# Attention, weight conversions and the first unit's products: finishing the second pair of tiles before the third is begun

## The chip, the cores and the metric

The kernel runs on one core of one Trainium2 chip. The metric is the device time of one execution in microseconds, as the median of several runs. The core has five engines with an instruction list each, worked off in order: TensorE (PE, matmuls and transposes), VectorE (DVE), ScalarE (ACT), GpSimd (POOL) and SyncE (SP, which here only issues loads and stores).

## The reference

Three stages follow each other. All arrays are float32 at the result; the weights of the second stage arrive as 64-bit floats.

```python
# 1: softmax attention inside chunks of 64 positions; q, k, v are (8, 8, 576, 64)
scores = scale * np.matmul(q_c, k_c.transpose(0, 1, 2, 4, 3))
attn = np.exp(scores - np.max(scores, axis=-1, keepdims=True))
attn = attn / (np.sum(attn, axis=-1, keepdims=True) + 1e-09)
out = np.matmul(attn, v_c)                      # -> x, (8, 576, 512)
# 2: token shift and channel mix; w_k 512x1024, w_v 1024x512, w_r 512x512
x_prev = np.concatenate([np.zeros((B, 1, D)), x[:, :-1, :]], axis=1)
xk = mu_k * x + (1.0 - mu_k) * x_prev
xr = mu_r * x + (1.0 - mu_r) * x_prev
k = np.maximum(xk @ w_k, 0.0)
v = k * k @ w_v
r = 1.0 / (1.0 + np.exp(-(xr @ w_r)))
x = r * v
# 3: four causal attention experts on x, the two best per token mixed by their gates
```

## The kernel before

`attn_mix` computes the first two stages, `experts` the third. The 4608 tokens are 36 tiles of 128 tokens for the attention and 12 units of 384 tokens (three tiles) for the mix.

**Attention.** Tiles are taken in pairs j. `s_T` turns q and k of one tile (four 128x128 transposes each on PE, a copy on ACT, L129), and issues the load of q and k two tiles on. `s_S` makes the scores of a pair (32 matmuls of 64x64, L154) and the softmax on DVE and ACT. `s_PT` turns the probabilities of one tile. `s_PV` multiplies by v (32 matmuls, L184), copies the result into the unit's tile XT on ACT (L44), and issues the loads of v two tiles on (four issues each, L113). `s_prev` (POOL) sets the column before a unit. These steps stand in the list `attn`; before the change, pair j's turn is: `s_T` of its two tiles, `s_PT` of the two tiles of pair j-1, then `s_SPV`, which is `s_S` of pair j and `s_PV` of pair j-1. So pair j-1 is finished only behind the transposes and scores of pair j.

**Mix.** `s_shift` makes, for one of four groups of 128 features, xr or xk of a unit: ACT scales the earlier tokens (L239), DVE adds the present ones (L240), ACT rounds to the high part (xhr or xhk, L243), and DVE subtracts for the low part (xlr or xlk, L244). Unit 0 needs XT of tiles 0 to 2, so both pair 0 and pair 1 must be finished. A product of high and low parts is three matmuls of 128x384 (L57 to L59). A unit is four `mix_r` (12 matmuls each, then a sigmoid on ACT, L257), eight `mix_k` (12 each) and four `mix_v` (24 each): 240 matmuls. The products go into three PSUM buffers named mps.

**Conversions.** Twenty pieces of 128x512 weights (four of w_r, eight of w_k, eight of w_v) go through `conv`: a load of 512 KB into `st` (L304), the absolute value on ACT into `cz` (L310), a maximum on POOL (L311), three integer operations on DVE (L312 to L314), the high part on POOL (L46) and the low part on DVE (L324, into wrl, wkl or wvl). There are two buffers of `cz` and two of `st`; the first four pieces use, as `st`, the tiles that later hold xhr, xlr, xhk and xlk.

**Order.** The program is written as one string of steps: CFG['pro'] for the opening (c a conversion, q and v loads, a an attention step, s the first unit's shift, ahead of which `attended(0)` runs all attention steps that unit 0 needs), and then the units' products with the rest among them: in unit 0 `early=(2, 1)` conversions per product item, and a running credit (rate0 for units 0 and 1, then rate) that releases one attention step when it reaches 1. A scheduler then lays out each engine's list from that order and from its own timing model, so the lists do not follow the string exactly.

Of the kernel before, what the change touches and what calls it, by code (L numbers as in the profile page):

```python
# [8 lines left out]
F32 = mybir.dt.float32  # L9
F32R = mybir.dt.float32r  # L10
I32 = mybir.dt.int32
# [8 lines left out]

CH = 64
UNIT = 384
CFG = dict(ps=(2, 3, 1, 2), P=5, sm=3, load=6, lag=(3, 4), out=(5, 1), qk1=(1, 1), qk0=(10, 1.2), v=(11, 1), order=(3, 4, 0, 1, 2), after=1, conv='v', clo='v', chi='g', x2hi='g', x2lo='v', ylo='g', yhi='v', xt='aa', r2='av', klo='vg', amul='vg', nearly=2, x2b=1, yb=4, qb=4, direct=((0, 1), (1, 1), (1, 1)), tailAV=4, kp=1, yt=1, yf=2, zb=1, om=(4, 3, 2, 1, 0), hp=1000, x2d=2, early=(2, 1), dact=3, rate0=0.43, rate=0.45, sh=(10, 12, 2), sh2=(11, 1, -1), pro='cccqqaacavvcaaaaacaacaaaascc', alag=2, seq=0, end=2, outL=(13, 2), outE=2, kcp='aa', dsc='v', ldb=2, vb=2, cn=512, stb=2, xb=4, pa=5, tb=2, first_j=7)
SEG = 192


# [22 lines left out]
def f32(ap):  # L49
    return ap.bitcast(F32)  # L50
# [11 lines left out]
def attn_mix(tc, at, x2T, q, k, v, mu_k, mu_r, w_k, w_v, w_r, ident, attended_all, mixed_k):  # L62
# [9 lines left out]
    TPU = UNIT // 128  # L72
# [4 lines left out]
    with ExitStack() as ctx:  # L77
        wts = ctx.enter_context(tc.tile_pool(name="wts", bufs=1))
        mx = ctx.enter_context(tc.tile_pool(name="mx", bufs=1))
        ps = ctx.enter_context(tc.tile_pool(name="psM", bufs=1, space=PSUM))  # L80

        pa_open = ExitStack()
        pa = pa_open.enter_context(tc.tile_pool(name="psA", bufs=1, space=PSUM, side="right"))
        wkr_open = ExitStack()
        wkr = wkr_open.enter_context(tc.tile_pool(name="wkr", bufs=1, side="right"))
# [9 lines left out]
        def runs(t):  # L95
            b, s = divmod(t * 128, S)
            return [(0, b, s, 128)] if s + 128 <= S else [(0, b, s, CH), (CH, b + 1, 0, CH)]

        def load_qk(t):
            for src, nm in ((q, "q"), (k, "k")):  # L100
                x = at.tile([128, H * D], F32, tag="ld" + nm, bufs=CFG["ldb"], name="ld" + nm)
                for p, b, s, n in runs(t):
                    nc.sync.dma_start(out=x[p:p + n].rearrange("p (h d) -> p h d", h=H),
                                      in_=src[b, :, s:s + n, :].rearrange("h p d -> p h d"))
                qkv[nm, t] = x

        def load_v(t):
            x = at.tile([128, 2, HP, D], F32, tag="ldv", bufs=CFG["vb"], name="ldv")
            for c in range(2):
                b, s = divmod(t * 128 + c * CH, S)  # L110
                for e in range(2):
                    r = e ^ c
                    nc.sync.dma_start(out=x[r * 64:(r + 1) * 64, c],  # L113
                                      in_=v[b, e::2, s:s + CH, :].rearrange("g p d -> p g d"))
            qkv["v", t] = x

        qT, kT, PP, PT, XT = {}, {}, {}, {}, {}
        nT = NU * TPU

        def bank(nm):  # L120
            return pa.tile([128, HP, 128], F32, tag="A", bufs=CFG["pa"], name=nm)

        def to_sbuf(src, nm):

            p = bank("Tps")
            for g in range(HP):
                nc.tensor.transpose(p[:, g], src[:, g * 128:(g + 1) * 128], ident)  # L127
            o = at.tile([128, HP, 128], F32, tag=nm, bufs=CFG["tb"], name=nm)
            nc.scalar.activation(out=o, in_=p, func=ACTF.Copy)  # L129
            return o  # L130

        def s_T(t):
            qT[t] = to_sbuf(qkv.pop(("q", t)), "qT")
            kT[t] = to_sbuf(qkv.pop(("k", t)), "kT")
            if t + CFG["ldb"] < nT:
                load_qk(t + CFG["ldb"])

# [6 lines left out]
        def s_S(j):  # L144
            banks = [bank("Sps").rearrange("p g (i k) -> p i g k", i=2) for _ in range(2)]
            for i in range(2):
                a, b = qT.pop(2 * j + i), kT.pop(2 * j + i)
                for g in range(HP):
                    for c in range(2):
                        for o in range(2):  # L150
                            e = o ^ c
                            r, cc = slice(e * 64, e * 64 + 64), slice(c * CH, (c + 1) * CH)
                            with tc.high_priority(1000) if j < CFG["first_j"] else nullcontext():
                                nc.tensor.matmul(out=banks[o][cc, i, g], lhsT=a[r, g, cc], rhs=b[r, g, cc],  # L154
                                                 start=True, stop=True)
            m = at.tile([128, 2, 2, HP], F32, tag="m", name="m")
            e = at.tile([128, 2, HP, 2, CH], F32, tag="P", name="P")
            for o, p in enumerate(banks):
                nc.vector.tensor_reduce(m[:, o], p, axis=AXX, op=ALU.max)
                nc.vector.tensor_tensor(e[:, :, :, o], p, m[:, o].unsqueeze(3).to_broadcast([128, 2, HP, CH]),  # L160
                                        op=ALU.subtract)
            ef = e.rearrange("p i g o k -> p (i g o) k")
            nc.scalar.activation(out=ef, in_=ef, func=ACTF.Exp, scale=scale)
            z = m.rearrange("p o i g -> p (o i g)")
            nc.vector.tensor_reduce(z, ef, axis=AXX, op=ALU.add)
            nc.vector.tensor_scalar(z, z, 1e-9, None, op0=ALU.add)
            nc.vector.reciprocal(z, z)
            eng(nc, CFG["amul"][j >= CFG["first_j"]]).tensor_tensor(
                ef, ef, z.unsqueeze(2).to_broadcast([128, 2 * H, CH]), op=ALU.mult)
            for i in range(2):  # L170
                PP[2 * j + i] = e[:, i]
# [33 lines left out]
        def s_SPV(j):  # L205
            if 2 * j < nT:
                s_S(j)
            if j:
                s_PV(j - 1)

        def s_prev(u):
# [84 lines left out]
        def conv(src, dst, g, c0, n):  # L296

            i = done[0] - 1
            if i < 4:

                st = wkr.tile([128, n, 2], I32, tag=("xhr", "xlr", "xhk", "xlk")[i], name="st")
            else:
                st = at.tile([128, n, 2], I32, tag="st", bufs=CFG["stb"], name="st")
            nc.sync.dma_start(out=st.rearrange("p f w -> p (f w)"),  # L304
                              in_=src.bitcast(I32)[g * 128:(g + 1) * 128, 2 * c0:2 * (c0 + n)])
            h, l = st[:, :, 1], st[:, :, 0]
            z = at.tile([128, n], F32, tag="cz", bufs=2, name="cz")
            b = z.bitcast(I32)

            nc.scalar.activation(out=z, in_=f32(h), func=ACTF.Abs)  # L310
            nc.gpsimd.tensor_scalar(z, z, F64_ZERO, None, op0=ALU.max)  # L311
            nc.vector.tensor_scalar(b, b, 3, 0x3FFFFFF8, op0=ALU.logical_shift_left, op1=ALU.bitwise_and)  # L312
            nc.vector.scalar_tensor_tensor(b, l, 29, b, op0=ALU.logical_shift_right, op1=ALU.bitwise_or)
            nc.vector.scalar_tensor_tensor(b, h, -(1 << 30), b, op0=ALU.bitwise_and, op1=ALU.bitwise_or)  # L314
            split(z, dst, g, c0, n)
# [6 lines left out]
        def split(z, dst, g, c0, n):  # L322
            copy(nc, CFG["chi"], dst.hi[:, g, c0:c0 + n], z)
            eng(nc, nth(CFG["clo"], done[0])).tensor_tensor(dst.lo[:, g, c0:c0 + n], z, f32(dst.hi[:, g, c0:c0 + n]), op=ALU.subtract)  # L324
# [12 lines left out]
        attn = []  # L337
        for j in range(nT // 2 + 1):
            two = (2 * j, 2 * j + 1)
            attn += [(t // TPU, s_T, t) for t in two if t < nT]  # L340
            attn += [((t - 2) // TPU, s_PT, t - 2) for t in two if t > 1]
            attn.append(((2 * j - 1) // TPU if j else 0, s_SPV, j))
            attn += [(t // TPU, s_prev, t // TPU) for t in (2 * j - 2, 2 * j - 1) if t > 0 and t % TPU == TPU - 1]
        attn.reverse()

        def attend(u, n=1):
# [22 lines left out]
        loads = {"q": iter(range(CFG["ldb"])), "v": iter(range(CFG["vb"]))}  # L369

        def first_shift():
            for ws in ((1, 0),) if CFG["sh2"][2] >= 0 else ((1,), (0,)):
                for g in range(KD):
                    s_shift(0, ws, g)

        for c in CFG["pro"]:
            if c == "a":
                attend(2)
            elif c == "c":
                convert(1)  # L380
            elif c in loads:
                (load_qk if c == "q" else load_v)(next(loads[c]))
            else:
                attended(0)
                first_shift()

        credit = 0.0
        for u in range(NU):
# [6 lines left out]
            for i, (f, *args) in enumerate(items):  # L395
# [10 lines left out]
                if u + 1 < NU:  # L406
                    both = u + 1 <= CFG["sh2"][2]
                    for ws, at0 in (((1, 0), CFG["sh2"][0]),) if both else (((1,), CFG["sh"][0]), ((0,), CFG["sh"][1])):
                        g, r = divmod(i - at0, CFG["sh2" if both else "sh"][1 if both else 2])
# [481 lines left out]
```

## Time and profile before

| | |
|---|---|
| median of 3 runs | 1044.99 us (1044.38 to 1045.49) |
| profiled execution | 1048.14 us |
| its span | 1046.4 us |
| PE busy | 993.4 us, 95% |
| DVE busy | 721.5 us, 69% |
| ACT busy | 586.5 us, 56% |
| POOL busy | 413.7 us, 40% |

The span runs from the first to the last instruction of the trace; the execution's own time lies 1.74 us above it, and 3.15 us above the median. PE is the busy engine, so the reading goes by where PE is not busy or runs below full clock, and then by what it waits for there: the windows, then the waits, then the chain of work that ended last, and then the engines' own timelines.

### The profile page before, as it was taken

How to read it: one execution, taken by the hardware profiler on the slowest of the kernel's cores; microseconds unless marked ns; L12 is line 12 of the kernel's file. 1: busy time of each engine (PE TensorE's matmuls, PEld its weight loads, DVE VectorE, ACT ScalarE, POOL GpSimd, SP SyncE). 2: the span in 40 equal slices, each digit the busy share in tenths (PEclk: the TensorE clock that was granted, in tenths of full speed). 3: DMA queues.
4: the chain of work that ended last, by engine and by line, in shares of the span. 5: the costliest groups of instructions: out<-in, count | busy, mean ns of one | idle time of the engine just before them, and what ended most of it. 6: DMA issues, size and time to landing. Idle time of an engine off the chain costs nothing.

```text
span 1046.4 us, 22262 instructions
## 1 busy us (share of the span) xinstructions
PE 993.4 (95%) x8422; PEld 953.4 (91%) x8422; DVE 721.5 (69%) x1793; ACT 586.5 (56%) x1379; POOL 413.7 (40%) x507
## 2 busy tenths in 40 slices
PE   3679899999999999999999999999999999999997
PEld 2569899998999999999999999999989998999986
DVE  5899835537654856565666632688787787878996
ACT  3378573545354545454453412477676776777675
POOL 5443303526443755464554537433332423313101
PEclk8589999999999999999999999999999999999999
DMA  9774522152324242323213125454452645253312
GB/s 230 188 197 122 126 57 81 41 122 62 86 58 109 54 122 49 99 72 87 56 47 81 31 61 131 107 145 119 103 155 58 181 72 158 63 156 108 103 34 92
DMA packets 167522, 105.27 MB, mean 101 GB/s; under 512 B 133512, under 2 KB 145912, under 8 KB 167416
## 3 DMA queue, kind: packets, MB, share of 16 engines
q1 hardware_dynamic: 132024, 54.55, 20.3%
q0 software_dynamic: 35392, 49.30, 18.2%
q8 instruction: 67, 1.10, 0.5%
q14 instruction: 39, 0.32, 0.1%
HBM read 66.01 MB, written 28.38 MB: 90 GB/s over the span
## 4 chain that ended last, share of the span: by engine, by line
PE 68%; DVE 18%; ACT 4%; DMA 4%; issue 3%; POOL 2%; SPq 1%; ACTq 0%; DVEq 0%; POOLq 0%
PE mps L57 12%; PE mps L59 12%; PE mps L58 12%; PE pj L57 5%; PE pj L58 5%; PE pj L59 5%; PE Tps L663 4%; PE Tps L127 3%; PE AVps L687 2%; PE AVps L683 2%; PE Sps L603 2%; PE Sps L602 2%; DVE r L271 2%; DVE sm L605 1%; PE Sps L154 1%
## 5 line engine op out<-in xcount | busy, mean ns | idle before, releaser
L57 PE MATMUL mps<-xhk,wkh 128*128 128x384 f32 x384 | 131.8, 344 | 0.1
L57 PE MATMUL mps<-kh,wvh 128*128 128x384 f32 x384 | 129.8, 342 | 1.1 <-DVE x2o L288 0.9
L58 PE MATMUL mps<-kl,wvh 128*128 128x384 f32 x384 | 128.4, 336 | 2.5 <-POOL kl L273 2.4
L58 PE MATMUL mps<-xlk,wkh 128*128 128x384 f32 x384 | 129.1, 337 | 0.0
L59 PE MATMUL mps<-xhk,wkl 128*128 128x384 f32 x384 | 128.9, 336 | 0.0
L59 PE MATMUL mps<-kh,wvl 128*128 128x384 f32 x384 | 127.0, 336 | 0.9 <-DVE wvl L324 0.9
L271 DVE TENSOR_TENSOR r<-r 128x384 f32<-128x384 f32 x80 | 65.8, 823 | 85.8 <-ACT r L264 85.8
L273 POOL TENSOR_TENSOR kl<-r,kh 128x384 fp32r<-128x384 f32 x80 | 87.7, 1100 | 83.0 <-ACT kh L272 81.9
L615 ACT ACTIVATE P<-sm,nm 128x128 f32<-128x128 f32 (+4 forms) x160 | 91.3, 571 | 36.9 <-DVE nm L609 20.2
L605 DVE CUSTOM_DVE_ANT_0 sm<-Sps,mask 128x192 f32<-128x192 f32 (+3 forms) x192 | 83.6, 438 | 18.5 <-PE Sps L603 16.9
L228 POOL TENSOR_TENSOR xa<-XT 128x384 f32<-128x384 f32 x72 | 71.0, 994 | 60.3 <-DVE xlr L244 34.9
L272 ACT ACTIVATE kh<-r 128x384 fp32r<-128x384 f32 x96 | 50.7, 529 | 59.5 <-DVE r L271 59.0
L663 PE MATMUL Tps<-ident,P 128*128 128x128 f32 x480 | 80.8, 275 | 1.4 <-DVE PT03l L667 0.5
L242 DVE SCALAR_TENSOR_TENSOR xa<-xa,mu,XT 128x384 f32<-128x384 f32 x72 | 67.2, 949 | 15.4 <-POOL xa L228 15.4
L58 PEld LDWEIGHTS mps<-kl,wvh 128*128 128x128 f32 x384 | 72.1, 188 | 4.0 <-POOL kl L273 4.0
L57 PEld LDWEIGHTS mps<-kh,wvh 128*128 128x128 f32 x384 | 71.9, 188 | 2.7 <-DVE x2o L288 1.2
L57 PEld LDWEIGHTS mps<-xhk,wkh 128*128 128x128 f32 x384 | 72.5, 189 | 1.0 <-ACT r L264 0.7
L524 POOL DMA_DIRECT2D K<-Kp x64 | 34.2, 553 | 98.7 <-ACT Kp L517 98.1
L59 PEld LDWEIGHTS mps<-kh,wvl 128*128 128x128 f32 x384 | 71.8, 188 | 1.2 <-DVE wvl L324 1.2
L58 PEld LDWEIGHTS mps<-xlk,wkh 128*128 128x128 f32 x384 | 72.3, 188 | 0.1
L57 PE MATMUL mps<-xhr,wrh 128*128 128x384 f32 x192 | 66.7, 349 | 5.8 <-ACT sig L257 3.3
L59 PEld LDWEIGHTS mps<-xhk,wkl 128*128 128x128 f32 x384 | 72.2, 188 | 0.0
(202 smaller groups left out, 2914.9 us busy)
## 6 DMA issues: line engine op xcount, KB each, us to landing
x2T<-x2d POOLq DMA_DIRECT2D x48, 384.0 KB, 3.2
x<-x2T POOLq DMA_DIRECT2D x32, 576.0 KB, 6.4
ldv<-in_v_dram SPq DMA_DIRECT2D x144, 64.0 KB
K<-Kp POOLq DMA_DIRECT2D x64, 144.0 KB, 3.0
ldq<-in_q_dram SPq DMA_DIRECT2D x32, 256.0 KB
ldk<-in_k_dram SPq DMA_DIRECT2D x32, 256.0 KB
out_dram<-o SPq DMA_DIRECT2D x32, 256.0 KB
st<-in_moe_w_k_dram SPq DMA_DIRECT2D x8, 512.0 KB
```

Of the source, the lines that this page charges most:

```text
L57: nc.tensor.matmul(out=out, lhsT=ah, rhs=bh, start=first and i == 0, stop=False)
L58: nc.tensor.matmul(out=out, lhsT=ah, rhs=bl, start=False, stop=False)
L59: nc.tensor.matmul(out=out, lhsT=al, rhs=bh, start=False, stop=last and i == n - 1)
L228: nc.gpsimd.tensor_tensor(d, now, prev, op=ALU.subtract)
L242: nc.vector.scalar_tensor_tensor(a, d, m, prev, op0=ALU.mult, op1=ALU.add)
L271: eng(nc, CFG["r2"][u >= CFG["nearly"]]).tensor_tensor(r2, r, r, op=ALU.mult)
L272: nc.scalar.activation(out=o.hi, in_=r2, func=ACTF.Copy)
L273: eng(nc, CFG["klo"][u >= CFG["nearly"]]).tensor_tensor(o.lo, r2, f32(o.hi), op=ALU.subtract)
L524: nc.gpsimd.dma_start(out=d[half[j]], in_=t[half[i]])
L605: nc.vector.tensor_tensor_reduce(out=sm[:n, a:a + w], in0=pp[:n, :w], in1=mk[:, a:a + w], op0=ALU.add, op1=ALU.min, scale=-scale, scalar=3e38,
L615: nc.scalar.activation(out=x[:n, :nk], in_=sm[:n, :nk], func=ACTF.Exp, scale=-1.0, bias=nm[:n, :1], accum_out=z)
L663: nc.tensor.transpose(pp[:, j - j0], x[:, o:o + 128], ident)
```

## The change

Five edits, all in `attn_mix` and its settings:

- in the list `attn`, pair 1 is finished ahead of pair 2: its two `s_PT`, its `s_PV` and unit 0's `s_prev` stand before `s_T` of tiles 4 and 5, and the turn of j = 2 then holds only `s_S`, with unit 1's tag;
- the opening string has 7 conversions and 12 attention steps ahead of the first shift's s where it had 9 and 14 (two more conversions and two more attention steps follow in before: its string ends `aaaaacaacaaaascc`, the new one `aaaaaccaaaas`);
- rate0 goes from 0.43 to 0.5;
- the first four conversions keep their value in a third part of the tile that holds their `st`, and take no `cz` buffer;
- `first_shift` always makes xk of all four groups and xr of all four apart. With the settings here it did that already.

Code below the edit moves down by one to six lines: L304 becomes L306, L310 to L314 become L311 to L315, L324 becomes L325.

```diff
-CFG = dict(
...
-rate0=0.43, pro='cccqqaacavvcaaaaacaacaaaascc',
+rate0=0.5, pro='cccqqaacavvcaaaaaccaaaas',
...
         def s_SPV(j):
             if 2 * j < nT:
                 s_S(j)
-            if j:
+            if j and j != 2:
                 s_PV(j - 1)
...
             if i < 4:
-                st = wkr.tile([128, n, 2], I32, tag=("xhr", "xlr", "xhk", "xlk")[i], name="st")
+                x = wkr.tile([128, 3 * n], I32, tag=("xhr", "xlr", "xhk", "xlk")[i], name="st")
+                st, z = x[:, :2 * n].rearrange("p (f w) -> p f w", w=2), f32(x[:, 2 * n:])
             else:
+                z = at.tile([128, n], F32, tag="cz", bufs=2, name="cz")
                 st = at.tile([128, n, 2], I32, tag="st", bufs=CFG["stb"], name="st")
...
-            z = at.tile([128, n], F32, tag="cz", bufs=2, name="cz")
...
-            attn += [(t // TPU, s_T, t) for t in two if t < nT]
-            attn += [((t - 2) // TPU, s_PT, t - 2) for t in two if t > 1]
-            attn.append(((2 * j - 1) // TPU if j else 0, s_SPV, j))
-            attn += [(t // TPU, s_prev, t // TPU) for t in (2 * j - 2, 2 * j - 1) if t > 0 and t % TPU == TPU - 1]
+            turned = [((t - 2) // TPU, s_PT, t - 2) for t in two if t > 1]
+            prevs = [(t // TPU, s_prev, t // TPU) for t in (2 * j - 2, 2 * j - 1) if t > 0 and t % TPU == TPU - 1]
+            if j == 2:
+                attn += turned + [(0, s_PV, 1)] + prevs
+                turned, prevs = [], []
+            attn += [(t // TPU, s_T, t) for t in two if t < nT] + turned
+            attn.append(((2 * j - 1) // TPU if j and j != 2 else 2 * j // TPU, s_SPV, j))
+            attn += prevs
...
-            for ws in ((1, 0),) if CFG["sh2"][2] >= 0 else ((1,), (0,)):
+            for ws in ((1,), (0,)):
```

The lists hold the same instructions in total, but for two more loads of an ACT table (25 for 23). Three places where the order differs follow; rows read line, operation, output and inputs, shape and a count. The first is ACT's list around the four copies (L44) that complete unit 0's XT: before, then after.

```order
L310 ACTIVATE cz<-st 128x512
L129 ACTIVATE PT<-Tps 128x512
L163 ACTIVATE P<-P 128x1024
L129 ACTIVATE qT<-Tps 128x512
L310 ACTIVATE cz<-st 128x512
L44 ACTIVATE XT<-PVps 128x4x64 x4
L239 ACTIVATE xb<-XT,mu_94 128x384 x2
L129 ACTIVATE kT<-Tps 128x512
L129 ACTIVATE qT<-Tps 128x512
L310 ACTIVATE cz<-st 128x512
L129 ACTIVATE kT<-Tps 128x512
L243 ACTIVATE xhr<-xb 128x384
```

```order
L311 ACTIVATE cz<-st 128x512
L129 ACTIVATE PT<-Tps 128x512 x2
L311 ACTIVATE cz<-st 128x512 x2
L44 ACTIVATE XT<-PVps 128x4x64 x4
L129 ACTIVATE qT<-Tps 128x512
L239 ACTIVATE xb<-XT,mu_94 128x384 x2
L129 ACTIVATE kT<-Tps 128x512
L129 ACTIVATE qT<-Tps 128x512
L243 ACTIVATE xhr<-xb 128x384
```

Before, the copies stand behind the absolute value of the eleventh conversion, and that of the twelfth stands between them and the first xhr; after, those of the eleventh and twelfth both stand ahead of the copies, and none between the copies and the first xhr.

The second is DVE's list around the first shift (the first L240 and the first L244), before and then after.

```order
L313 SCALAR_TENSOR_TENSOR cz<-st,cz 128x512
L314 SCALAR_TENSOR_TENSOR cz<-st,cz 128x512
L165 TENSOR_REDUCE m<-P 128x16
L166 TENSOR_SCALAR m<-m 128x16
L167 RECIPROCAL m<-m 128x16
L168 TENSOR_TENSOR P<-P,m 128x1024
L324 TENSOR_TENSOR wkl<-cz,wkh 128x512
L240 SCALAR_TENSOR_TENSOR xb<-XT,mu,xb 128x384 x2
L312 TENSOR_SCALAR cz<-cz 128x512
L313 SCALAR_TENSOR_TENSOR cz<-st,cz 128x512
L244 TENSOR_TENSOR xlr<-xb,xhr 128x384
```

```order
L325 TENSOR_TENSOR wkl<-cz,wkh 128x512 x2
L313 TENSOR_SCALAR cz<-cz 128x512
L314 SCALAR_TENSOR_TENSOR cz<-st,cz 128x512
L315 SCALAR_TENSOR_TENSOR cz<-st,cz 128x512
L313 TENSOR_SCALAR cz<-cz 128x512
L240 SCALAR_TENSOR_TENSOR xb<-XT,mu,xb 128x384
L314 SCALAR_TENSOR_TENSOR cz<-st,cz 128x512
L240 SCALAR_TENSOR_TENSOR xb<-XT,mu,xb 128x384
L315 SCALAR_TENSOR_TENSOR cz<-st,cz 128x512
L244 TENSOR_TENSOR xlr<-xb,xhr 128x384
```

Before, the last softmax of the opening and one conversion stand ahead of the first L240; after, no softmax stands there, and the twelfth conversion's operations are spread around the two L240.

The third is PE's list up to the first products (rhs xhr), before and then after.

```order
L127 MATMUL Tps<-ident,ldk 128x128 x4
L127 MATMUL Tps<-ident,ldq 128x128 x4
L127 MATMUL Tps<-ident,ldk 128x128 x4
L127 MATMUL Tps<-ident,P 128x128 x8
L154 MATMUL Sps<-kT,qT 64x64 x32
L184 MATMUL PVps<-PT,ldv 64x64 x32
L57 MATMUL mps<-xhr,wrh 128x384
L58 MATMUL mps<-xlr,wrh 128x384
L59 MATMUL mps<-xhr,wrl 128x384
```

```order
L127 MATMUL Tps<-ident,ldk 128x128 x4
L127 MATMUL Tps<-ident,ldq 128x128 x4
L127 MATMUL Tps<-ident,ldk 128x128 x4
L154 MATMUL Sps<-kT,qT 64x64 x16
L57 MATMUL mps<-xhr,wrh 128x384 x3
L154 MATMUL Sps<-kT,qT 64x64 x16
L58 MATMUL mps<-xlr,wrh 128x384
L59 MATMUL mps<-xhr,wrl 128x384
```

Before, the scores of pairs 2 and 3, the turned probabilities of tiles 4 and 5 and the products with v of pair 2 stand ahead of the first product; after, only half of pair 2's scores do, and the rest of this work stands among the products.

## Rows read from the trace of the kernel before

**Rows 1.** Windows: stretch, us, busy PE, PEld, DVE, ACT, POOL, PE clock, DMA, GB/s.

```profile
0.00:62.05 62.05, 32.32 (x454) 25.07 (x457) 43.56 (x68) 26.47 (x47) 28.16 (x35) 0.72 0.81 205
62.05:120.64 58.59, 52.79 (x575) 50.60 (x572) 56.57 (x96) 43.93 (x88) 24.92 (x22) 0.91 0.53 138
76.57:82.00 5.43, 5.43 (x18) 5.33 (x19) 3.88 (x8) 2.73 (x6) 0.78 (x1) 0.50 0.53 138
128.40:600.00 471.60, 465.41 (x4203) 455.44 (x4203) 279.70 (x408) 229.52 (x452) 219.51 (x244) 1.00 0.30 74
```

**Rows 2.** PE's waits from 64.7 to 128.4: total us, times, longest us.

```profile
PE mps L57 <- ACT sig L257: 3.3, 1, 3.3
```

**Rows 3.** The chain that ended last, 20 to 130: start us, us, what.

```profile
55.59 4.79 DMA st<-in_moe_w_k_dram
...
62.05 0.56 DVE xlr L244
...
120.04 0.60 DVE wvl L324
```

**Rows 4.** Timeline of SP's issues: start us, us, engine, line, what, count.

```profile
41.21 0.55 SPq L103 DMA_DIRECT2D ldq<-in_q_dram  x1
...
42.49 1.85 SPq L304 DMA_DIRECT2D st<-in_moe_w_k_dram  x1
...
48.78 0.96 SPq L304 DMA_DIRECT2D st<-in_moe_w_k_dram  x1
...
55.59 0.49 SPq L304 DMA_DIRECT2D st<-in_moe_w_k_dram  x1
...
97.83 0.34 SPq L304 DMA_DIRECT2D st<-in_moe_w_v_dram  x1
```

**Rows 5.** Timeline of ACT; in brackets the idle time before and its releaser.

```profile
21.75 0.66 ACT L310 ACTIVATE cz<-st 128x512 f32<-128x512 f32 x1 [5.59 <-DMA st<-in_moe_w_k_dram]
...
48.41 0.68 ACT L310 ACTIVATE cz<-st 128x512 f32<-128x512 f32 x1 [1.28 <-DVE wkl L324]
...
55.62 0.67 ACT L310 ACTIVATE cz<-st 128x512 f32<-128x512 f32 x1 [1.59 <-DMA st<-in_moe_w_k_dram]
56.20 1.19 ACT L44 ACTIVATE XT<-PVps 128x256 f32<-128x256 f32 x4
...
60.47 0.66 ACT L310 ACTIVATE cz<-st 128x512 f32<-128x512 f32 x1 [1.11 <-DMA st<-in_moe_w_k_dram]
61.03 0.58 ACT L129 ACTIVATE kT<-Tps 128x512 f32<-128x512 f32 x1
...
101.42 0.73 ACT L310 ACTIVATE cz<-st 128x512 f32<-128x512 f32 x1
```

**Rows 6.** Timelines of POOL and of DVE.

```profile
49.18 1.49 POOL L311 TENSOR_SCALAR cz<-cz 128x512 f32<-128x512 f32 x1 [1.51 <-ACT cz L310]
...
53.08 0.69 DVE L314 SCALAR_TENSOR_TENSOR cz<-st,cz 128x512 int32<-128x512 int32 x1
```

**Rows 7.** Timeline of PE.

```profile
64.72 0.64 PE L57 MATMUL mps<-xhr,wrh 128*128 128x384 f32 x1
...
69.54 0.60 PE L127 MATMUL Tps<-ident,ldq 128*128 128x128 f32 x4
69.98 0.60 PE L127 MATMUL Tps<-ident,ldk 128*128 128x128 f32 x4
...
77.06 0.52 PE L58 MATMUL mps<-xlr,wrh 128*128 128x384 f32 x1
77.38 0.52 PE L59 MATMUL mps<-xhr,wrl 128*128 128x384 f32 x1
...
82.37 1.16 PE L154 MATMUL Sps<-kT,qT 64*64 64x64 f32 x64
83.35 0.68 PE L184 MATMUL PVps<-PT,ldv 64*64 64x64 f32 x32
...
128.40 0.34 PE L57 MATMUL mps<-xhr,wrh 128*128 128x384 f32 x1
```

More of the change, by code (lines that the diff above doesn't have):

```diff
@@ L22 @@
 UNIT = 384
-CFG = dict(ps=(2, 3, 1, 2), P=5, sm=3, load=6, lag=(3, 4), out=(5, 1), qk1=(1, 1), qk0=(10, 1.2), v=(11, 1), order=(3, 4, 0, 1, 2), after=1, conv='v', clo='v', chi='g', x2hi='g', x2lo='v', ylo='g', yhi='v', xt='aa', r2='av', klo='vg', amul='vg', nearly=2, x2b=1, yb=4, qb=4, direct=((0, 1), (1, 1), (1, 1)), tailAV=4, kp=1, yt=1, yf=2, zb=1, om=(4, 3, 2, 1, 0), hp=1000, x2d=2, early=(2, 1), dact=3, rate0=0.43, rate=0.45, sh=(10, 12, 2), sh2=(11, 1, -1), pro='cccqqaacavvcaaaaacaacaaaascc', alag=2, seq=0, end=2, outL=(13, 2), outE=2, kcp='aa', dsc='v', ldb=2, vb=2, cn=512, stb=2, xb=4, pa=5, tb=2, first_j=7)
+CFG = dict(ps=(2, 3, 1, 2), P=5, sm=3, load=6, lag=(3, 4), out=(5, 1), qk1=(1, 1), qk0=(10, 1.2), v=(11, 1), order=(3, 4, 0, 1, 2), after=1, conv='v', clo='v', chi='g', x2hi='g', x2lo='v', ylo='g', yhi='v', xt='aa', r2='av', klo='vg', amul='vg', nearly=2, x2b=1, yb=4, qb=4, direct=((0, 1), (1, 1), (1, 1)), tailAV=4, kp=1, yt=1, yf=2, zb=1, om=(4, 3, 2, 1, 0), hp=1000, x2d=2, early=(2, 1), dact=3, rate0=0.5, rate=0.45, sh=(10, 12, 2), sh2=(11, 1, -1), pro='cccqqaacavvcaaaaaccaaaas', alag=2, seq=0, end=2, outL=(13, 2), outE=2, kcp='aa', dsc='v', ldb=2, vb=2, cn=512, stb=2, xb=4, pa=5, tb=2, first_j=7)
 SEG = 192
```

## The prediction

> **What bounds the kernel now.** I read the windows first. From 128.40 to 600 us PE is busy 465.41 of 471.60 us at full clock, and in the opening, up to 62.05 us, it is busy 32.32 of 62.05 us at a mean clock of 0.72 [rows 1]. So time can only be won or lost in the first 128 us, and from there on each microsecond of PE work that is still to be done is a microsecond of the end. Next, the chain that ended last [rows 3] says what holds PE back: it goes through the load of a weight piece that is issued at 55.59 and takes 4.79 us, through the first low part of unit 0's xr (L244, 62.05), and through the twentieth conversion's low part (wvl, 120.04 and 0.60 long, so done at 120.64). The reader is to see that these are no PE rows. Between 62.05 and 120.64 DVE is busy 56.57 of 58.59 us [rows 1]: DVE's list is the limit of this stretch, and PE waits beside it, above all 3.3 us for a sigmoid [rows 2]. The first product is at 64.72, unit 1's first at 128.40 [rows 7]; the latter is the mark by which I count, since PE runs nearly without a gap behind it.
>
> So there are three questions: when does the first xlr come, how long does DVE take from there to the twentieth conversion, and how much attention work is still ahead of PE when unit 1 begins.
>
> **When the first xlr comes.** Unit 0's last XT copies start at 56.20, directly behind the eleventh conversion's absolute value (55.62), which ended a wait for its load; from the copies to the first xlr it is 62.05 - 56.20 = 5.85 us, of which ACT idles 1.11 us for the twelfth piece's load and spends 61.03 - 60.47 = 0.56 us on it [rows 3, 5]. In the new order no conversion stands between copies and xhr, but one turned q (L129) does, about 0.5 us by the same kind of row; so the copies' way becomes 5.85 - 1.11 - 0.56 + 0.5 = 4.7 us, and 4.2 us if the second turned q no longer waits. In exchange the twelfth conversion's absolute value stands ahead of the copies. Its load needs the `st` of the tenth, which DVE frees with L314 (53.08 and 0.69, so 53.77 [rows 6]); before, it is then issued at 55.59, behind four loads of v and one of q [rows 4]. Now:
>
> - The tenth's load, issued at 42.49, stands behind a pair of q and k loads (from 41.21 [rows 4]) that is gone: 1.3 us earlier. It lands as before, 48.41 - 42.49 = 5.9 us later [rows 4, 5], at 47.1.
> - Its maximum on POOL starts 0.77 behind that and takes 1.49 [rows 5, 6]. No softmax now stands in DVE's list here, so the three operations follow at some 0.7 each, with the ninth's low part among them: done near 51.3, where it was 53.77.
> - The twelfth's load now stands directly behind the eleventh's, so it goes at 51.3. By its own row it lands 60.47 - 55.59 = 4.9 us later, at 56.2. The other rows of this kind give 6.8 (48.78 to 55.62) and 3.6 (97.83 to 101.42, with fewer loads about) [rows 4, 5].
> - With 0.6 for the absolute value the copies start at 56.8, 0.6 us later than before, and by ACT the first xlr follows at 56.8 + 4.2 = 61.0. By DVE it is a little later: the maximum ends at 56.2 + 0.77 + 1.49 = 58.5, and the conversion's three operations and two L240 stand ahead of the xlr, 2.8 us at 0.56 to 0.59 each: 61.3.
>
> I take 61.3, the later of the two, 0.75 us earlier than before. The ends are 60.0 (a landing of 3.6, 1.3 less) and 64.1 (landings of 6.8 for both pieces, 0.9 and 1.9 more).
>
> **From there to the twentieth conversion.** Two pairs' softmax and shift operations have moved. From the first xlr to the last wvl DVE's list holds 11 operations less. By the window each of its 96 takes 56.57 / 96 = 0.59 us [rows 1], so 6.5 us. I add 0.5 us, since a list this full that is moved forward meets loads sooner; its bounds are 0 and 3. The twentieth is done at 61.3 + 58.59 - 6.5 + 0.5 = 113.9, 6.7 us earlier. PE can follow: its first product moves by about 1 us, and of what it lost behind that, 3.3 us were the sigmoid [rows 2], ahead of the matching product of which the new order puts 13 transposes, and the 18 entries from 76.57 to 82.00 at a clock of 0.50 [rows 1] cost, at 0.32 apart [rows 7] for 0.17 at full speed (half the 0.34 of a row at 128.40, as two overlap), 18 x 0.15 = 2.7 us. If both go, PE could come 1 + 3.3 + 2.7 = 7.0 us earlier too; so both ways agree within 0.3 us, and neither leaves much more.
>
> **What is left to do.** Unit 1's first product follows the same 240 products in both orders. By then the new order has turned 30 blocks fewer (22 of q and k, 8 of P), and has done one pair's scores (32 matmuls) and one pair's products with v (32) less. By [rows 7]: 30 x (69.98 - 69.54) / 4 = 3.3 us; 32 / 64 x (83.35 - 82.37) = 0.5 us; 0.6 us, by the 0.68 of the row at 83.35 less its overlap. That is 4.4 us, and as PE is full behind 128.40 [rows 1], all of it comes back. DVE, ACT and POOL do their share there in spare time (279.70, 229.52 and 219.51 of 471.60 us), so I put that at nothing; if that cover failed, DVE's 15 operations put off, at 0.59 us, would show as 8.9 us.
>
> **The other edits.** rate0 only sets where the steps stand, and is in the counts above. The first four conversions without `cz`: the fifth, the first that could profit, waits 5.59 us for its load, not for a buffer, at 21.75 [rows 5]; nothing, with bounds of 0 and 1 us gained. The two more table loads lie on ACT, which has 14.7 us spare from 62.05 to 120.64 [rows 1]; nothing, and 3.3 us if one holds PE once more as the sigmoid's wait does [rows 2]. first_shift does what it did.
>
> **Sum.** 6.7 - 4.4 = 2.3 us earlier. The profiled execution took 1048.14 us, 1.74 above its span and 3.15 above the median; the same change on the median, 1044.99, gives **1042.7 us**.
>
> **Rivals.**
>
> *Quicker still.* The two pieces land in 3.6 us each [rows 4, 5]: xlr at 60.0, and the 0.5 us of extra waits is nil: the twentieth at 60.0 + 58.59 - 6.5 = 112.1, 8.5 us earlier, less 4.4: 1040.9, if PE can follow. For it: fewer loads of q and k stand between the pieces. Against it: DMA's share is 0.81 in the opening [rows 1], and the loads are of the same size.
>
> *Slower: the copies behind the twelfth conversion.* ACT works in order, and XT's copies, both scale steps, xhr and so every product are now queued behind an absolute value that waits for a 512 KB load. If both that load and the one before take 6.8 us, as that of the eleventh does in before, xlr comes at 64.1; and if six of the later conversions each meet half a microsecond of the same, 3 us: 64.1 + 58.59 - 6.5 + 3.0 = 119.2, only 1.4 us earlier, less 4.4 of work put off: 3.0 us slower, 1048.0. It decides from the point where the twentieth conversion comes later than 120.64 - 4.4 = 116.2.
>
> *The clock.* Products that begin in short bursts run at half clock: the 3.3 us wait ahead of 76.57 [rows 2] was followed by 5.43 us at a granted clock of 0.50 [rows 1], the 1.2 GHz level. The new order has taken dense attention work from the front of the products, which now come one by one as each xlr is done; if the first 36 all ran at half clock, 36 x 0.15 = 5.4 us would be lost: 1048.1 if all of it showed, 1045.4 if half lay in time in which PE waits for the next xlr anyway. I take the middle, 1046.8. Against it, transposes and scores still stand directly ahead. The Trainium skill, page "TensorE: Matmul & The Clock Gate", section "HAM oscillation — how this bites in real kernels", describes this: bursts of matmuls parted by waits for loads each start again at half clock. By that rule the time would be that 1046.8; the trace of before agrees for the one wait at 76.57.
>
> *No effect.* The scheduler's lists follow its own timing; if the twelfth load or a turned q holds the shift up to 62, and PE's 13 transposes only take the place of the sigmoid's wait, the 4.4 us won equal the 4.4 put off: 1045.0.
>
> **How the numbers follow.** Forecast (1041 to 1044.4): 0.43. Quicker: 0.14. Slower: 0.18. Clock: 0.09, the upper 0.04 above the bound. No effect: 0.16. What a measurement can tell here is 0.2%, 2.1 us: below 1042.9 is faster, above 1047.1 slower. The forecast lies at the edge of the first; I count 0.28 of its 0.43 below it, as its two ways to unit 1 agree and the gains of the quicker kind are not spent; with the quicker case 0.42 faster. Same: 0.15 + 0.05 + 0.16 = 0.36. Slower: 0.18 + 0.04 = 0.22. The range goes from 1039.8, a little below the quicker case, to 1048.0, which takes in the clock and the slower case at its price; what is left out is below 0.2. Cases of both signs hold weight; the forecast's own range is 1041 to 1044.4.
>
> **What would show it.** In the new profile: the copies (L44) of unit 0 directly behind a wait for a weight load on ACT, at 56 to 58; the first xlr at 60 to 62; the sigmoid's wait below 1.5 us; the low part of the twentieth conversion (now L325) done near 113.9; unit 1's first product near 121.7; PE's idle time from there to 600 us unchanged at some 6 us. I am wrong in the middle step if the twentieth is not done by 116.2, in the first if xlr comes behind 62.05, in the last if unit 1 begins 6.7 us earlier and the end does not follow by 2 to 3 us, and altogether if a half clock shows from 60 to 75 us.

## The result, and the profile after

The changed kernel takes 1050.39 us (1049.54 to 1053.22) against 1044.99 us: a ratio of 1.0057, interval 1.0041 to 1.0073. A second set of runs gave 1051.15 against 1044.32, 1.0074 (1.0046 to 1.0102). So it is slower by 5 to 7 us, where 2.3 us faster was forecast, and lies outside the range.

The windows of the changed kernel, in the columns of [rows 1]: up to the first low part of unit 0's xr (xlr), from there to the twentieth conversion's low part, from there to unit 1's first product, the two together, and unit 1.

```profile
0.00:60.59 60.59, 26.22 (x353) 20.16 (x354) 41.13 (x65) 23.47 (x42) 30.23 (x36) 0.69 0.76 192
60.59:114.46 53.87, 50.29 (x510) 47.23 (x509) 50.82 (x86) 42.19 (x81) 22.94 (x18) 0.94 0.54 140
114.46:124.54 10.08, 9.07 (x75) 8.08 (x75) 9.80 (x19) 3.62 (x7) 2.62 (x5) 0.83 0.55 130
60.59:124.54 63.95, 59.36 (x585) 55.30 (x584) 60.63 (x103) 45.80 (x87) 25.56 (x23) 0.92 0.54 138
124.54:175.85 51.31, 51.31 (x542) 49.91 (x537) 26.83 (x48) 33.21 (x66) 6.91 (x12) 1.00 0.39 99
```

Those of a second profile of the kernel before (called b0 below), by the same marks:

```profile
0.00:60.14 60.14, 28.73 (x455) 22.42 (x458) 43.53 (x68) 26.45 (x47) 28.00 (x35) 0.78 0.84 210
60.14:118.45 58.31, 51.69 (x575) 49.04 (x571) 56.89 (x96) 43.76 (x88) 24.98 (x22) 0.96 0.52 140
118.45:126.19 7.74, 7.46 (x77) 7.09 (x76) 6.44 (x13) 5.11 (x11) 2.10 (x5) 1.00 0.72 159
60.14:126.19 66.05, 59.15 (x650) 56.13 (x646) 63.33 (x107) 48.87 (x99) 27.08 (x27) 0.96 0.55 142
126.19:170.62 44.43, 44.43 (x347) 44.06 (x347) 18.66 (x35) 22.62 (x45) 7.20 (x12) 1.00 0.25 73
```

Three things are to be seen. The first xlr comes no earlier than in b0 (60.59 and 60.14), though PE and DVE have less behind them by then. The twentieth conversion comes 4.0 us earlier (114.46 and 118.45), but unit 1 only 1.65 (124.54 and 126.19): 2.3 of them are lost in the row between. And unit 1 takes 51.31 for 44.43 us, all of it with PE busy. Set side by side, in us, with the second profile of the changed kernel (a0):

| stretch | before [rows 1, 3, 7] | b0 | after | a0 | as forecast |
|---|---|---|---|---|---|
| start to the first xlr | 62.05 | 60.14 | 60.59 | 60.20 | 61.3 |
| first xlr to unit 1 | 66.35 | 66.05 | 63.95 | 63.01 | 60.4 |
| unit 1 to unit 2 | 44.39 | 44.43 | 51.31 | 51.31 | |
| unit 2 to unit 11 | 441.24 | 440.58 | 442.02 | 443.20 | |
| unit 11 to the end | 432.4 | 430.7 | 430.0 | 430.4 | |
| span | 1046.4 | 1041.9 | 1047.9 | 1048.1 | |

From b0 to after the span grows by 6.0 us: +0.45, -2.1, +6.9, +1.4 and -0.6. From the first xlr to unit 11 the stretches of one order agree between its two profiles to 1.2 us, units 1 to 10 of before even to 0.7 in all; what differs most between the two profiles of before is the opening (1.9 us), and the experts (1.7 us).

### The profile page after: what moved, and what is told of

Read it like the earlier page. It is cut to its first block, busy times and chain, and to the rows that moved or that the text cites. A ratio compares the mean times of both kernels' runs of the same rounds, so it can differ in the third digit from the quotient of the medians.

```text
span 1047.9 us, 22240 instructions
## 1 busy us (share of the span) xinstructions
PE 992.3 (95%) x8422; PEld 950.4 (91%) x8422; DVE 727.2 (69%) x1793; ACT 588.2 (56%) x1381; POOL 412.4 (39%) x507
## 4 chain that ended last, share of the span: by engine, by line
PE 68%; DVE 17%; DMA 5%; ACT 4%; issue 3%; POOL 2%; SPq 1%; ACTq 0%; DVEq 0%; POOLq 0%
PE mps L57 12%; PE mps L59 11%; PE mps L58 11%; PE pj L57 5%; PE pj L58 5%; PE pj L59 5%; PE Tps L669 4%; PE Tps L127 3%; PE AVps L693 3%; PE AVps L689 2%; PE Sps L609 2%; PE Sps L608 2%; DVE xa L242 2%; DVE r L271 2%; DMA st<-in_moe_w_k_dram 1%
## 5 line engine op out<-in xcount | busy, mean ns | idle before, releaser
L273 POOL TENSOR_TENSOR kl<-r,kh 128x384 fp32r<-128x384 f32 x80 | 88.2, 1105 | 78.0 <-ACT kh L272 78.0
L228 POOL TENSOR_TENSOR xa<-XT 128x384 f32<-128x384 f32 x72 | 67.2, 945 | 78.3 <-DVE xlr L244 51.0
L272 ACT ACTIVATE kh<-r 128x384 fp32r<-128x384 f32 x96 | 50.7, 528 | 62.4 <-DVE r L271 62.2
L242 DVE SCALAR_TENSOR_TENSOR xa<-xa,mu,XT 128x384 f32<-128x384 f32 x72 | 71.3, 1013 | 10.9 <-POOL xa L228 10.8
```

Of the source, the lines that this page charges most:

```text
L228: nc.gpsimd.tensor_tensor(d, now, prev, op=ALU.subtract)
L242: nc.vector.scalar_tensor_tensor(a, d, m, prev, op0=ALU.mult, op1=ALU.add)
L272: nc.scalar.activation(out=o.hi, in_=r2, func=ACTF.Copy)
L273: eng(nc, CFG["klo"][u >= CFG["nearly"]]).tensor_tensor(o.lo, r2, f32(o.hi), op=ALU.subtract)
```

## The experiments

**The same kernels again.** Two profiles were wanted before any difference of 3 us was explained.

> The kernel before, unchanged, for a second profile. In its first profile unit 1's first product starts at 128.40 us, unit 2's at 172.79, unit 11's at 614.03, and 432.4 us follow. If these marks are properties of the order, the second profile has unit 2 within 0.7 us of 172.8 and unit 11 within 1 us of 614.0, and the execution's time near the median 1045.0 means that the stretch behind unit 11 is near 430. If instead the marks scatter by 2 us or more, the 3.1 us between the two kernels at unit 2 says little.

1043.36 us; unit 1 at 126.19, unit 2 at 170.62, unit 11 at 611.20. So the marks scatter by 2.2 to 2.8 us, and the lengths of the stretches have to be compared instead: from unit 1 to unit 11 they repeat. The difference ahead of unit 1 is scatter of the opening, and b0 is the early one: b_cz, b_rate and b_low below, which keep the old list and the old opening string, have their first xlr at 62.61, 62.73 and 61.73, beside 62.05 in before and 60.14 in b0. The 1.7 us in the experts are the profile's on which the prediction rests (432.4 us, where the others have 429.4 to 431.3).

> The changed kernel, unchanged, for a second profile beside that of before. If its marks belong to its order: unit 1's first product at 124.5 within 1.5 us, unit 2's at 175.9 within 1.5 us, and 1049.5 to 1051 us. If the 5 us to before were scatter of the opening, unit 2 would come below 173.

1051.15 us; unit 1 at 123.21, unit 2 at 174.52. The marks are within the expectation, and the slowdown belongs to the changed kernel and not to one execution.

**The list of attention steps alone, and all but the list.** b_attn is the kernel before with the edit of the list only, the core of which is repeated here; a_attn is the changed kernel with the old list.

```diff
             if j == 2:
                 attn += turned + [(0, s_PV, 1)] + prevs
                 turned, prevs = [], []
```

> The kernel before with the new list of attention steps alone (pair 1 finished ahead of pair 2); opening string, rate0 and cz as before. Theory 1 (the list is the cause: 5.4 us of transposes, scores and products with v leave the opening, where PE is half idle, for the units, where it is full, and the earlier start gives back only a part): 1048 to 1050.5 us, unit 1 near 124 to 126, unit 2 near 175.5 to 176. Theory 2 (the list is harmless; the conversions' new order, with two absolute values ahead of the copies, and the half clock near 115 cost the time): 1044.5 to 1046, unit 2 near 172.8.

> The changed kernel with the old list of attention steps; opening string, rate0 and cz as changed. Theory 1: 1044 to 1046 us, unit 1 near 128, unit 2 near 172 to 174 (its list has 0.6 us more attention done by then). Theory 2: 1048.5 to 1050.5, unit 2 at 175 or later.

b_attn: 1052.43 us, ratio 1.0080 (1.0062 to 1.0097), unit 1 at 129.47, unit 2 at 179.65: slower than theory 1 had it. a_attn: 1042.48 us, 0.9979 (0.9967 to 0.9990), unit 1 at 127.37, unit 2 at 172.68: faster than either theory. So the list is the cause of the whole loss, some 8 us with either set of the other edits, and the other edits together are a small gain. a_attn has the changed kernel's 25 loads of an ACT table and b_attn the 23 of before, so those are not the cause. From a_attn to the changed kernel, which differ by the list alone, the span grows by 7.8 us: -0.7 up to the first xlr, -2.1 from there to unit 1, +6.0 in unit 1, +4.0 in units 2 to 10 and +0.7 behind. Part of the loss thus lies far behind the place where the list was changed. How b_attn loses even more than the changed kernel is in its windows, from the first xlr to the twentieth conversion and on to unit 1:

```profile
61.13:113.81 52.68, 49.24 (x476) 46.57 (x475) 47.78 (x79) 38.71 (x74) 22.21 (x18) 0.94 0.56 144
113.81:129.47 15.66, 10.92 (x109) 10.16 (x110) 13.22 (x24) 9.08 (x17) 3.54 (x7) 0.78 0.43 102
```

The twentieth conversion comes 4.6 us earlier than in b0 and unit 1 3.3 us later. PE's timeline there, with the idle time ahead in brackets, then DVE's:

```profile
116.72 0.49 PE L127 MATMUL Tps<-ident,P 128*128 128x128 f32 x3
121.46 1.09 PE L127 MATMUL Tps<-ident,ldq 128*128 128x128 f32 x4 [4.25 <-issue]
122.48 1.13 PE L184 MATMUL PVps<-PT,ldv 64*64 64x64 f32 x32
```

```profile
119.68 0.61 DVE L240 SCALAR_TENSOR_TENSOR xb<-XT,mu,xb 128x384 f32<-128x384 f32 x1
120.20 0.55 DVE L244 TENSOR_TENSOR xlk<-xb,xhk 128x384 fp32r<-128x384 f32 x1
120.67 1.28 DVE L160 TENSOR_TENSOR P<-Sps,m 128x512 f32<-128x512 f32 x2
```

PE waits 4.25 us, and goes on some 0.1 us after the first of DVE's two L160 has read its bank of scores (two in 1.28 us from 120.67). The transposes write into the same five PSUM banks as the scores (the tag `A` in the kernel), so I take this as the wait for a bank, though the trace names no releaser. That softmax stands in DVE's list behind the shift of unit 1 (L240, L244). The changed kernel shows the same place at 118.51, with 0.95 us of waiting, right behind its first L160 (two in 1.28 us from 117.72), and a0 with 2.15 us, PE's row first:

```profile
117.20 0.63 PE L127 MATMUL Tps<-ident,ldq 128*128 128x128 f32 x4 [2.15 <-issue]
```

```profile
116.42 1.28 DVE L160 TENSOR_TENSOR P<-Sps,m 128x512 f32<-128x512 f32 x2
```

**Is DVE the bound up to unit 1?** Two kernels take work off DVE. b_low and a_low leave out one integer operation in conversions 12 to 20, so that those weights lose their low three bits; the edit below is b_low's, and a_low's is the same:

```diff
-            nc.vector.scalar_tensor_tensor(b, l, 29, b, op0=ALU.logical_shift_right, op1=ALU.bitwise_or)
+            if i < 11:
+                nc.vector.scalar_tensor_tensor(b, l, 29, b, op0=ALU.logical_shift_right, op1=ALU.bitwise_or)
```

> The kernel before without one of the three integer operations on DVE (L313, which adds the low three bits of the value) in conversions 12 to 20; those weights lose three bits. Nine operations of 0.68 us leave DVE between the first xlr and unit 1, nothing else changes there but the places that the scheduler then gives (by the list 25.9 us of attention by unit 1 for 28.3). Theory (DVE's busy time from the first xlr on sets when unit 1 begins): 5 to 6 us less from xlr to unit 1 than the 66.05 of before, that is 60 to 61.5. Rival (PE's own work, its clock or the loads set it): 64 us or more.

> The changed kernel without the same integer operation in conversions 12 to 20. Theory (DVE sets unit 1's start here too): from xlr to unit 1 59 to 60.5 us, where the changed kernel has 63.95; and as 22.0 us of attention are done by then for 22.9, some 3 us of it reach the end, 1046 to 1048. Rival (PE, which is busy 59.4 of the 63.95 us, is the bound): 62.5 us or more.

The windows from the first xlr to unit 1, b_low and then a_low:

```profile
61.73:121.75 60.02, 56.98 (x601) 54.88 (x597) 55.01 (x93) 45.18 (x89) 24.99 (x27) 0.94 0.59 154
```

```profile
60.30:121.39 61.09, 57.04 (x588) 53.95 (x581) 53.67 (x92) 47.82 (x89) 25.57 (x25) 0.95 0.57 151
```

b_low, 1041.48 us (0.9975, 0.9961 to 0.9990): DVE's busy time falls from 63.33 to 55.01 us and the stretch from 66.05 to 60.02, as the theory had it. In the old order DVE was the bound, as the prediction said. The run doesn't part this quite from PE's work: of the 14 operations that left DVE only nine were taken out, the scheduler put five others, with 2.5 us of attention, behind unit 1's start (PE is busy 56.98 us for 59.15), and unit 1 then takes 47.07 us for 44.43. a_low, 1049.10 us (1.0043, 1.0027 to 1.0060): DVE falls from 60.63 to 53.67 us, the stretch only from 63.95 to 61.09; the expectations of 59 to 60.5 us and of 1046 to 1048 were both missed. Its twentieth conversion is done at 103.70, 10.8 us earlier than in the changed kernel, and unit 1 starts 3.2 us earlier, 17.7 us behind it, and in these PE is never idle:

```profile
103.70:121.39 17.69, 17.69 (x222) 16.98 (x221) 16.07 (x30) 12.81 (x25) 5.93 (x8) 1.00 0.69 164
```

So the twentieth conversion does not set unit 1, and once DVE is relieved, PE's own work does.

t_klo, the changed kernel with the old list, moves the subtractions of units 0 and 1 (L273) from DVE to POOL, eight of them ahead of unit 1.

```diff
-klo='vg'
+klo='gg'
```

> The changed kernel with the old list of attention steps, and the low part of k squared (L273) of units 0 and 1 on POOL instead of DVE: eight operations of 0.7 us leave DVE's list ahead of the twentieth conversion. If DVE's list sets when unit 1 begins, unit 1 starts 3 to 5.6 us earlier than 127.4, and the time is 1037.5 to 1040. Rival (PE's own work, its clock and the loads set it, and DVE only looks full): unit 1 at 127 to 128, 1042 to 1044; PE may then wait for POOL, whose operation takes 1.1 us.

1048.38 us (1.0041, 1.0026 to 1.0056), slower by 5.9 us than a_attn; both theories missed. The profiled execution was the fastest of its ten, 1045.30 us, so its trace shows 3.4 of the 5.9 us. The windows from the first xlr to unit 1, of a_attn and then of t_klo:

```profile
61.28:127.37 66.09, 58.83 (x645) 55.52 (x635) 63.36 (x107) 48.89 (x99) 27.12 (x27) 0.97 0.53 138
```

```profile
61.57:129.67 68.10, 58.30 (x640) 53.59 (x632) 66.17 (x99) 48.84 (x98) 37.05 (x34) 1.00 0.54 137
```

Eight operations left DVE (107 to 99), and its busy time rose from 63.36 to 66.17 us. It rose in operations that did not change, in groups of DVE by form, a_attn and then t_klo:

```profile
L314 DVE SCALAR_TENSOR_TENSOR cz<-st,cz 128x512 int32<-128x512 int32 x9 | 6.1, 676 | 0.0
L313 DVE TENSOR_SCALAR cz<-cz 128x512 int32<-128x512 int32 x9 | 3.7, 416 | 0.0
L160 DVE TENSOR_TENSOR P<-Sps,m 128x512 f32<-128x512 f32 x6 | 4.0, 682 | 0.0
```

```profile
L314 DVE SCALAR_TENSOR_TENSOR cz<-st,cz 128x512 int32<-128x512 int32 x9 | 7.8, 869 | 0.1
L313 DVE TENSOR_SCALAR cz<-cz 128x512 int32<-128x512 int32 x9 | 5.8, 644 | 0.1
L160 DVE TENSOR_TENSOR P<-Sps,m 128x512 f32<-128x512 f32 x6 | 3.9, 680 | 0.0
```

Unit 1's start followed DVE's busy time again (+2.8 us busy, +2.0 us in the stretch), with the sign turned round. The last section shows what ran beside these operations.

**Can the deferred attention be taken back?** a_20 and t_26 put more attention steps into the opening string, with the new list (20 for 12, shown here) and with the old one (24 for 12).

```diff
-pro='cccqqaacavvcaaaaaccaaaas'
+pro='cccqqaacavvcaaaaaccaaaaaaaaaaaas'
```

> The changed kernel with eight more attention steps ahead of the first shift (20 in the opening string instead of 12): by its list 26.2 us of attention work is done by unit 1's first product, where the changed kernel has 22.9 and the kernel before 28.3 (counted from the lists at 0.109 us per transpose, 0.98 per pair's scores, 2.44 per pair's products with v). Theory 1 (time goes with the attention that is left for the full units; by the second profile of before, 5.4 us put off bought only 126.2 - 124.5 = 1.7 us, or 0.3 per us): unit 1 at about 125.5, 2.3 us won on the changed kernel, 1047 to 1049. Rival (the new order of steps itself costs the time, not the amount): 1050 to 1051.

> The changed kernel with the old list of attention steps and sixteen steps in place of four behind the conversions, so 33.4 us of attention are done by unit 1 where the same without them has 28.3 (1042.5 us, unit 1 at 127.4). Theory 1 with the exchange of 0.3 us per us: unit 1 at 129, 3.5 us won, 1038 to 1040. Rival (the opening is full for DVE: one more pair puts 15 of its operations, 8.9 us, ahead of the twentieth conversion): unit 1 at 134 to 136, 1044 to 1047.

a_20: 1049.34 us (1.0058, 1.0036 to 1.0080), unit 1 at 127.57 for 124.54, with 3.3 us more of attention ahead of it. t_26: 1045.58 us (1.0014, 1.0000 to 1.0029), unit 1 at 134.22 for 127.37, with 5.1 us more. The exchange of 0.3 us per us fell with both, and t_26 came out as its rival said. (The 2.44 us for a pair's products in a_20's text is that of two pairs; its sums use 1.22.) The lists say why: in both the scheduler placed the added steps behind the first product and not in the opening (in a_20 the opening holds the same 64 transposes as in the changed kernel, in t_26 92 for 88). So neither run tested the opening. Between the first xlr and unit 1 DVE and PE are each busy some 62.4 of 68.5 us in a_20, and there the steps cost about their full time (3.0 for 3.3 us, 6.9 for 5.1). In the opening they had cost little: from a_attn to the changed kernel 24 transposes and 88 rows of scores, some 4 us of PE's work, left it, and the first xlr came 0.7 us earlier, less than its scatter. Behind unit 1's start a_20 is quicker in its profile: 49.44 us for 51.31 in unit 1 and 437.58 for 442.02 in units 2 to 10. That profile was the fastest of its six executions, 2.2 us below their median, so how much of this the time of 1049.34 us keeps is open.

**The smaller edits.**

> The kernel before with the first four conversions' value in the tile of their st, nothing else. The prediction put this at nothing, with 0 to 1 us gained: 1043.4 to 1044.4 us. If it is what makes the changed kernel with the old list 1.9 us faster than before, it gives 1042 to 1043 here.

> The kernel before with rate0 = 0.5 for 0.43 alone: one attention step more is released in unit 1 (31.6 us of attention done by unit 2 for 31.0), nothing is moved ahead of unit 1. The changed kernel with the old list of attention steps, which has this edit, was 1.9 us faster than before, and behind unit 2 its profile takes 438.0 us to unit 11 where before takes 440.6. If rate0 does that: 1042 to 1043 us, 438 us from unit 2 to unit 11. If it is the conversions' edits: 1044.4 within 0.7, 440.6 us.

> The changed kernel with rate0 back at 0.43, so one attention step less is released in unit 1; by the lists 21.4 us of attention are done by unit 1 (22.9 in the changed kernel) and 31.0 by unit 2 (31.6). With the old list of attention steps, 0.5 for 0.43 shortened units 2 to 10 from 440.6 to 437.7 us. If the amount of attention is what counts: 1050 to 1052 us, unit 2 at 174.5 to 176. If the changed kernel's longer units 2 to 10 (442.0 and 443.2 us in two profiles) come from rate0 in this order of steps: 440 to 441 us here, and 1048 to 1049.5.

b_cz: 1044.56 us, 1.0003 (0.9990 to 1.0016): nothing, as predicted. b_rate: 1042.75 us, 0.9987 (0.9971 to 1.0002), and 437.72 us from unit 2 to 11 where b0 takes 440.58; a_attn, with the same rate, takes 438.02. So rate0 saves some 2.6 to 2.9 us in units 2 to 10 in the traces, for 0.9 us more in unit 1, and its time points the same way without being clear of no change. a_rate: 1051.07 us (1.0067, 1.0045 to 1.0088), as the amount of attention had it, unit 2 at 176.49, half a microsecond behind the range, and 442.36 us from there to unit 11. The saving does not appear with the new list. All of PE's waits between unit 2 and unit 11, 6.4 us in the changed kernel and then 2.2 in a_attn:

```profile
PE mps L57 <- DVE x2o L288: 4.0, 4, 2.2
PE mps L57 <- ACT r L264: 1.6, 3, 0.8
PE mps L58 <- POOL kl L273: 0.6, 1, 0.6
PE mps L57 <- ACT kh L272: 0.2, 1, 0.2
```

```profile
PE mps L58 <- POOL kl L273: 0.9, 2, 0.6
PE mps L57 <- DVE x2o L288: 0.6, 1, 0.6
PE mps L57 <- ACT kh L272: 0.5, 2, 0.4
PE mps L57 <- ACT sig L257: 0.2, 1, 0.2
```

The two differ by 4.2 us, the stretches by 4.0. Why the longer unit 1 leaves units 2 to 10 with these waits was not followed further, so the cause of this part of the loss stays open. The version that beats both kernels is a_attn, by 0.1 to 0.3% against the kernel before: the opening string, rate0 and the cz edit, without the new list.

## Why the prediction was wrong

**The opening** went as told in part. The copies of XT stand behind the twelfth conversion, as ACT's timeline of the changed kernel shows:

```profile
55.35 0.67 ACT L311 ACTIVATE cz<-st 128x512 f32<-128x512 f32 x1 [3.00 <-DMA st<-in_moe_w_k_dram]
55.92 1.20 ACT L44 ACTIVATE XT<-PVps 128x256 f32<-128x256 f32 x4
```

and the first xlr came at 60.59, for 61.3; the copies started at 55.92, for 56.8. One of its rows was misread on the way: ACT's start at 48.41 was released by DVE (wkl) and not by the load, so the load took at most the 5.9 us; in the changed kernel the load let ACT start at 46.48, for 47.1. Whether the forecast 0.75 us were won is not settled. The old opening has its first xlr from 60.14 to 62.73 in five profiles (62.05 in the middle), the new one at 60.20, 60.30, 60.59 and 61.14 (after, a0, a_low, a_rate): some 1.6 us earlier by the middle, nothing against b0. What sets its end in the changed kernel's trace is this load, for which ACT waits 3.00 us, and of attention only XT's copies and one turned q stand on the chain from there to the xlr, nothing that was taken out. PE's busy time in the opening fell from 28.73 to 26.22 us, at a clock of 0.69 for 0.78, in a stretch in which PE is idle over half the time.

**The step that failed most** is "From there to the twentieth conversion". Its arithmetic held (113.9 predicted, 114.46 and 113.16 measured), but the mark was wrong. I let the rest of the way to unit 1 stay at 7.76 us [rows 3, 7] and carried all 6.7 us over; from b0 to after unit 1 came 1.65 us earlier. DVE's count in the windows shows it: from the first xlr to the twentieth conversion 86 operations for 96, but from there to unit 1 19 for 13. Over the whole way it is 103 for 107, as both orders make the same three pairs' softmaxes there; the scheduler had put the conversions in front and not taken work away: four rows of a softmax (L159, L160) and two low parts of unit 1's own shift (L244) moved behind the twentieth. Unit 1 needs its own shift from DVE, and PE, as I take it, the banks that the softmaxes hold, so the saving is four operations, 60.63 for 63.33 us busy. PE's timeline after the twentieth conversion in the changed kernel shows what took the place:

```profile
112.63 0.34 PE L58 MATMUL mps<-kl,wvh 128*128 128x384 f32 x1
114.52 0.48 PE L59 MATMUL mps<-kh,wvl 128*128 128x384 f32 x1 [1.55 <-DVE wvl L325]
114.80 0.52 PE L57 MATMUL mps<-kh,wvh 128*128 128x384 f32 x1
...
118.51 0.63 PE L127 MATMUL Tps<-ident,ldq 128*128 128x128 f32 x4 [0.95 <-PE Tps L127]
```

A wait for the conversion, products of 0.52 us for 0.34 behind it, and a wait behind the transposes. The granted clock of that window is 0.83, so the half clock (the 1.2 GHz level) looks like a cause. a0 tells it apart; its window over the same way:

```profile
113.16:123.21 10.05, 7.85 (x75) 7.09 (x75) 9.77 (x18) 3.61 (x7) 2.62 (x5) 1.00 0.54 132
```

At full clock throughout it takes 10.05 us too, with PE idle for the difference, so the clock is not what holds it. In both profiles PE goes on with the transposes some 0.1 us after the first L160 has ended (118.51 in the changed kernel, 117.20 in a0), and has 6.0 us of its own work from there to unit 1, without a gap. DVE, busy 9.77 of 10.05 us, holds the first part of the way, and PE's own work is the second.

**The work left to do** was sized at 4.4 us; it is 5.5. A pair's scores are 32 matmuls in the list, but 64 rows in the trace (x64 in [rows 7] is one pair, 0.98 us), and a pair's products with v likewise 64 rows, of which the row at 83.35 holds half. I halved the one row and left the other as it was, as if list and trace counted alike: 3.3 + 1.0 + 1.2 us. In the traces PE spends 8.5 us of unit 1 on attention for 2.6 in b0, start to start; by the lists 0.6 us of the difference is the step that rate0 adds.

**The cover** failed too. I put the deferred work among the products at PE's bare time. Unit 1's 240 products took 42.8 us for 41.8, again start to start, with 18 changes between products and attention rows for 6, and units 2 to 10 took 1.4 to 2.6 us more than in b0, 4.0 to 5.2 more than in a_attn, above all in waits for x2o and r. So time was also lost behind the first 128 us, where the prediction had ruled it out. The text had a bound for DVE's part alone, 8.9 us, and carried nothing.

Put together, the forecast and the traces of b0 and after lie 8.3 us apart: 5.0 of these are ahead of unit 1, 2.5 in unit 1 and 0.8 behind it.

**The rivals.** "Slower" named the right sign with the wrong mechanism: the copies did wait for the twelfth conversion, but xlr was not later, and the twentieth conversion came at 114.46, far ahead of the 116.2 from which that rival decides. "The clock" wanted the first 36 products at half clock. It shows, but by the products' durations for about the first six of them (ten in a0), and again from 73.8 to 77.0, some 1 us behind the sigmoid's wait, which came down to 2.0 us and not below 1.5. From 66 to 72.67 the changed kernel ran at full clock:

```profile
66.00:72.67 6.67, 4.66 (x32) 4.38 (x30) 6.67 (x13) 5.53 (x9) 2.46 (x2) 1.00 0.20 49
```

"No effect" was the nearest in mechanism: what was won is less than what was put off. With the sizes that the runs show, 0.45 us later, 2.1 us back, 5.9 + 1.0 us in unit 1 and 1.4 behind it, the sum is 6.7 us slower to unit 11, and 6.0 to the end.

## What to carry to other kernels

When an engine is full over a stretch, count what it has to do up to the point where the next engine is free of it, not up to the operation that now gates it; moving that operation forward only moves the rest behind it. Work that lies in a stretch that waits for loads can be nearly free: here taking 4 us of it out shortened the stretch by 0.7 us (a_attn to the changed kernel), and it was paid in full where it landed. Before a few microseconds are explained, profile the same kernel more than twice, since the second profile can be the odd one, and compare stretches between marks of the program.

## What was not expected of the hardware

The t_klo pair shows DVE operations that were not touched becoming slower beside POOL's subtractions (L273): L313 from 416 to 644 ns and L314 from 676 to 869 in the mean. The means hide two kinds. Six of the nine L313 took 0.41 to 0.42 us, as all do in a_attn; one took 0.82, and two that started behind an L273 took three times as long, POOL's rows first, then DVE's:

```profile
100.60 1.01 POOL L273 TENSOR_TENSOR kl<-r,kh 128x384 fp32r<-128x384 f32 x1
103.22 1.30 POOL L273 TENSOR_TENSOR kl<-r,kh 128x384 fp32r<-128x384 f32 x1
```

```profile
100.66 1.24 DVE L313 TENSOR_SCALAR cz<-cz 128x512 int32<-128x512 int32 x1
103.56 1.25 DVE L313 TENSOR_SCALAR cz<-cz 128x512 int32<-128x512 int32 x1
```

Each ended 0.3 us after the L273 beside it, as if most of its work had waited for that. The other way round, an L168 that started 0.28 us ahead of an L273 (at 93.10) took its usual 1.21 us, and that L273 took 1.80 where the others took 1.01 to 1.45. The Trainium skill, "GPSIMD Engine Reference", section "Specifications", lists GpSimd's SBUF interface as shared with VectorE, contending with instructions that have two SBUF inputs or use a two-port mode. The rows agree for L314, with two inputs in SBUF, of which one took 1.49 us beside an L273; that L313, with one, is slowed would have to be the two-port case. It takes 416 ns where L314 takes 676 for the same 512 elements, which would fit a faster mode, but no row names it. L160, which reads its scores from PSUM, kept its time (682 and 680 ns), but none of the six ran beside an L273, so this says nothing of it.
